# Deadlines of spread-out work that follow TensorE's lag, and the last output chunk computed at the very end in two halves

## The chip, the cores and the metric

The kernel runs on one core of one Trainium2 chip. The metric is device time in microseconds (us) for one execution of the whole program. A core has five engines that work side by side, each through its own queue of instructions in a fixed order: TensorE (PE in the profile, with its weight loads as PEld), VectorE (DVE), ScalarE (ACT), GpSimd (POOL) and SyncE (SP), which here only issues DMA transfers. An instruction that waits for another engine holds up everything behind it in its own queue.

## The reference

For a sequence of 2048 rows with 640 channels, the input is normalised by rows, and three things are added: the input, a state-space convolution of the normalised rows, and a dense layer with a Mish activation.

```
xn = layernorm(x)                                   # x: 2048 x 640
y  = causal_convolution(xn, K) + xn * D_skip        # K from A, C, dt: one kernel per channel
h  = xn @ w1 + b1                                   # w1: 640 x 1728
act = h * tanh(softplus(h))                         # Mish
return x + y + act @ w2                             # w2: 1728 x 640
```

## The kernel before

**Blocks, chunks and products.** The 2048 rows are handled in 4 blocks of 512 (`b` = 0 to 3), the 1728 hidden channels in 14 chunks (`f` = 0 to 13: 128 channels each, chunk 8 only 64), the 640 output channels in 5 chunks of 128 (`k` = 0 to 4). Every float32 product is made of three products of 16-bit parts (high by high, low by high, high by low). For each block and chunk TensorE makes the hidden values (`mm1`, matmul line L770), ACT and DVE turn them into activations (`chain`), and TensorE multiplies them with `w2` and adds them up in five banks `ACC[k]` (`mm2`, L822, 15 matmuls of 512 columns for a full chunk), three chunks later.

**Pairs.** In blocks 1 to 3 chunks (0,1), (2,3), (4,5), (6,7), (9,10) and (11,12) are made in pairs by a scheme with fewer products (`mm1_pair`, L790, matmuls of 256 columns). For each pair TensorE runs five pieces, `one`, `two`, `three_a`, `three_b` and `four`, with pieces of older `mm2` between them. `three_a` (9 matmuls) needs a sum that DVE makes in PSUM (`z`, L1022), `four` needs another (`w`, L1026); ACT makes two copies between `one` and `two` (L1018, L1019). "Pair 3/4" below is the pair of block 3 that begins with chunk 4.

**The chain of a chunk.** Sigmoid (ACT L852), product with it (DVE L856), arctan, square and tanh (ACT L861, L866, L871), product (DVE L876), high part (ACT L883), low part (DVE L894).

**Spread work.** Between all this lies work that is due only much later: the normalisation and splitting of the next block (L621, L535, L580, L587), the convolution as two scans on DVE for each of 5 channel chunks of a block (copies on ACT L706 and L708, scans L712 and L716, sum L726: `ka`, `kb`, `kc`, `ke` in the planner), and 29 checks on the size of the weights (`ck`, ACT L672 and L675, with their loads `lc` on SP). The checks end in a chain of small DVE instructions (`ce`, L682 to L694), a small product on TensorE in the middle of pair 3/9 (L697), and a flag (L700).

**The planner.** The class `Plan` sets the order of instructions on every engine while the program is being built. TensorE's operations stand in one fixed list; each of them is due when the operations before it would end if TensorE never waited (`dues`). Operations of the other engines inherit deadlines backwards from those that need them; spread work also carries an explicit deadline (`due=`). `run` then gives each engine, again and again, the ready operation with the earliest deadline.

**The end.** After the last `mm1` (chunk 13 of block 3) come the `mm2` of chunk 10, then `t 0` (9 matmuls of chunk 11), `t 1` (15 of chunks 11 and 12), and `tail`, which needs chunk 13's activations. In `tail` each output chunk gets its last products, is added to the rows by DVE (`drain`, L899) and stored from SP (L900). Output chunk 4 gets chunk 13's products last, in two halves of 256 columns in two other banks; its bank is added to the rows before that (L1055). SP waits for all stores before the program ends (L1314).

Of the kernel before, what the change touches and what calls it, by code (L numbers as in the profile page):

```python
# [17 lines left out]
OP = mybir.AluOpType  # L18
AX = mybir.AxisListType

P = 128
# [4 lines left out]
TB = 512  # L26
NB = L // TB
NT = TB // P
KD = D // P
FC = [P] * 8 + [64] + [P] * 5  # L30
# [29 lines left out]
class Plan:  # L60
# [26 lines left out]
    def add(self, name, eng, cost, fn, pre=(), take=None, drop=(), due=None, rel=0.0, kb=0.0):  # L87
        assert name not in self.ops, name
        self.ops[name] = o = dict(name=name, eng=eng, cost=cost, fn=fn, pre=[p for p in pre if p not in self.end],
                                  take=take, drop=drop, due=1e9 if due is None else due, rel=rel, kb=kb, n=len(self.ops))  # L90
        if eng == "PE":
            self.pe.append(o)

# [13 lines left out]
    def dues(self):  # L107
        t = self.t["PE"]
        for o in self.pe:
            o["due"] = t + o["cost"]  # L110
            t += o["cost"]
        order, seen = [], set()

        def visit(o):
            stack = [(o, iter(o["pre"]))]
            seen.add(o["name"])
            while stack:
                x, it = stack[-1]
                p = next(it, None)
                if p is None:  # L120
                    order.append(x)
                    stack.pop()
                elif p not in seen:
                    seen.add(p)
                    stack.append((self.ops[p], iter(self.ops[p]["pre"])))

        for o in self.ops.values():
            if o["name"] not in seen:
                visit(o)
        for o in reversed(order):  # L130
            for p in o["pre"]:
                q = self.ops[p]
                if q["eng"] != "PE":
                    wait = 4.0 if q["kb"] else self.GAP[q["eng"]]
                    q["due"] = min(q["due"], o["due"] - o["cost"] - wait)

    def run(self):
        self.dues()
        todo = {e: {} for e in self.t}
        for o in self.ops.values():  # L140
            todo[o["eng"]][o["name"]] = o
        line = list(self.pe)
        while any(todo.values()):
            best = None
            for e, ops in todo.items():
                if not ops:
                    continue
                c = []
                for o in ([line[0]] if e == "PE" else ops.values()):
                    r = self.ready(o)  # L150
                    if r is not None:
                        c.append((max(r, self.t[e]), o))
                if not c:
                    continue
                t0 = min(r for r, _ in c)
                now = sorted((o["due"] - o["cost"], o["n"], o) for r, o in c if r <= t0 + 1e-9)
                late = [(o["due"] - o["cost"], r, o) for r, o in c if r > t0 + 1e-9]
                pick = None
                for u, _, o in now:
                    if not any(w < u and r < t0 + o["cost"] and w < t0 + o["cost"] for w, r, _ in late):  # L160
                        pick = (t0, o)
                        break
                if pick is None:
                    _, r, o = min(late, key=lambda z: (z[1], z[0]))
                    pick = (r, o)
                if best is None or pick[0] < best[0]:
# [253 lines left out]
def body(ctx: ExitStack, tc: tile.TileContext, x, xT, logA, Aim, Cr, Ci, logdt, vec, w1, w1T, w2, w2T, out):  # L420
# [378 lines left out]
    def mm2_ops(f, ks=range(KD), end=False):  # L799
        n = FC[f]  # L800
        hi, lo = ACT[f]
        st, en = f == 0, f == LAST or end
# [15 lines left out]
        return [t for x, y, z in zip(h, m, l) for t in ((*x, False, False), (*y, False, False), (*z, False, en))]  # L818

    def run(ops):  # L820
        for o, w, x, start, stop in ops:
            pe.matmul(o, w, x, start=start, stop=stop)  # L822

    def mm2(f, ks=range(KD), end=False):
        run(mm2_ops(f, ks, end))

    def mm2_last(ks, t=slice(0, TB), to=None):

        hi, lo = (z[:, t] for z in ACT[LAST])
        o = [(ACC[k] if to is None else to)[:, t] for k in ks]  # L830
        for k, z in zip(ks, o):
            c = slice(k * P, (k + 1) * P)
            pe.matmul(z, W2H[LAST][:, c], hi, start=to is not None, stop=False)
            pe.matmul(z, W2L[LAST][:, c], hi, start=False, stop=False)
        for k, z in zip(ks, o):
            pe.matmul(z, W2H[LAST][:, k * P:(k + 1) * P], lo, start=False, stop=True)


    def src(b, f):
# [62 lines left out]
    def whole():  # L902
# [31 lines left out]
        def second(b, f, parts):  # L934
# [7 lines left out]
            for j, (lo, hi) in enumerate(zip([0, *parts], ends)):  # L942
                last = j == len(parts)

                def go(lo=lo, hi=hi):
                    run(mm2_ops(f)[lo:hi])

                more = []
                if f == 0 and b > 0:
                    more = [[("j", b - 1, 0), ("j", b - 1, 1)], [("j", b - 1, k) for k in (2, 3, 4)], []][j]  # L950
                cost = M5 * (min(hi, 15) - lo) if FC[f] == P else 0.17 * (hi - lo)
                ops.append(lambda name=("m2", *n, j), go=go, p=pre + more, d=[("h", *n)] if last else [], cost=cost: add(
                    name, M, cost, go, pre=p, drop=d))
            return ops
# [31 lines left out]
        for b in range(1, NB):  # L986
            for f in range(NF):
# [45 lines left out]
                if i == NP - 1 and b == NB - 1:  # L1033
# [6 lines left out]


        b, k = NB - 1, KD - 1
        add(("t", 0), M, 9 * M5, lambda: mm2(LAST - 2, [4, 3, 2]), pre=[("a4", b, LAST - 2), ("v4", b, LAST - 2)])
        add(("t", 1), M, 15 * M5, lambda: (mm2(LAST - 1, [4], end=True), mm2(LAST - 1, [3]), mm2(LAST - 2, [0]),
                                           mm2(LAST - 1, [0]), mm2(LAST - 2, [1])),
            pre=[("a4", b, LAST - 1), ("v4", b, LAST - 1)])

        def tail(b=NB - 1, k=KD - 1):
# [11 lines left out]
        add(("t", 2), M, 30 * M5, tail, pre=[("a4", b, LAST), ("v4", b, LAST)] + [("ex", b, j) for j in range(KD)])  # L1060


        at = {}
# [277 lines left out]
```

## Time and profile before

| | |
|---|---|
| median of 3 executions | 366.23 us (365.05 to 366.76) |
| the profiled execution | 364.73 us, its span 362.9 us |
| granted TensorE clock | 0.998 |
| busy: PE / DVE / ACT / POOL | 351.1 / 311.4 / 298.3 / 48.8 us |
| chain that ended last | PE 86%, DVE 7%, DMA 3%, ACT 2% |

The span runs from the first to the last instruction; the 1.8 us by which the execution is longer lie outside it. A row of waits names the engine and line that waited, what it waited for, and the total, the count and the longest in us. A row of windows gives, for a stretch of the span, the busy us of each engine. TensorE is busy nearly all the time, so what counts is where it waits, and what lies before its first matmul and behind its last.

### The profile page before, as it was taken

Reading aid. Unit: us, or ns where it says so; the run is one execution under the profiler, and the core shown is the slowest. Engines: PE = TensorE matmul, PEld = TensorE weight load, DVE = VectorE, ACT = ScalarE, POOL = GpSimd, SP = SyncE. Lnnn points to the kernel's source line nnn. Section 1 sums busy time; section 2 is a strip of 40 time slices with the busy share of each in tenths; the row PEclk is TensorE's granted clock in tenths of the full one; section 3 lists DMA queues with packets and bytes.
Section 4 is the critical chain, followed back from the end, with each engine's and each line's share of the span. In section 5 each row is a group of like instructions: output and inputs, shape, how many; then the busy total and the mean of one; then the engine's idle time right before and its main releaser. Section 6 shows DMA issues by size and latency. Waiting matters only on the chain.

```text
span 362.9 us, 6023 instructions
## 1 busy us (share of the span) xinstructions
PE 351.1 (97%) x2161; PEld 210.7 (58%) x2161; DVE 311.4 (86%) x585; ACT 298.3 (82%) x614; POOL 48.8 (13%) x72
## 2 busy tenths in 40 slices
PE   7999999999999999999999999999999979999992
PEld 6754444445666665665666665576556646566541
DVE  5989989999998999999999867999999688885443
ACT  3599999987488699899989797999889986977730
POOL 2100010000032201020104231010003630000000
PEclk9999999999999999999999999999999999999999
DMA  7879975105129908622447942932003973111004
GB/s 231 279 235 286 349 233 189 54 1 181 38 47 194 327 37 209 252 65 54 122 155 153 239 135 64 345 93 67 0 2 58 177 189 72 29 29 31 0 4 151
DMA packets 26037, 48.75 MB, mean 134 GB/s; under 512 B 3577, under 2 KB 6929, under 8 KB 26001
## 3 DMA queue, kind: packets, MB, share of 16 engines
q1 hardware_dynamic: 19152, 34.21, 29.5%
q0 software_dynamic: 6240, 13.11, 17.8%
q10 hardware_dynamic: 608, 0.98, 0.8%
q8 instruction: 19, 0.31, 0.4%
q14 instruction: 18, 0.14, 0.2%
HBM read 39.10 MB, written 5.26 MB: 122 GB/s over the span
## 4 chain that ended last, share of the span: by engine, by line
PE 86%; DVE 7%; DMA 3%; ACT 2%; issue 1%; ACTq 0%
PE acc L822 43%; PE h L790 17%; PE h L770 13%; PE tr L790 10%; DMA w<-in_w_dram 3%; PE h L752 1%; PE tr L752 1%; DVE xl L535 1%; DVE A L856 1%; DVE g L716 1%; DVE lo L894 1%; DVE g L712 1%; DVE tl L587 1%; DVE A L876 0%; DVE t L580 0%
## 5 line engine op out<-in xcount | busy, mean ns | idle before, releaser
L822 PE MATMUL acc<-hi,w2h 128*128 128x512 f16 x275 | 101.6, 379 | 0.0
L822 PE MATMUL acc<-hi,w2l 128*128 128x512 f16 (+1 forms) x267 | 100.5, 379 | 0.0
L822 PE MATMUL acc<-lo,w2h 128*128 128x512 f16 x255 | 94.0, 379 | 0.0
L822 PEld LDWEIGHTS <-w2h 128*128 128x128 f16 x530 | 51.6, 98 | 48.9 <-issue 1.3
L790 PEld LDWEIGHTS <-w1h 128*128 128x128 f16 x432 | 42.3, 98 | 10.7
L852 ACT ACTIVATE s<-h,cv 128x512 f32<-128x512 f32 (+1 forms) x51 | 30.7, 604 | 20.9 <-PE h L790 16.1
L822 PEld LDWEIGHTS <-w2l 128*128 128x128 f16 x275 | 25.8, 98 | 31.3 <-issue 1.6
L876 DVE SCALAR_TENSOR_TENSOR A<-p,A 128x512 f32<-128x512 f32 (+1 forms) x56 | 38.3, 684 | 5.9 <-ACT p L871 5.6
L894 DVE SCALAR_TENSOR_TENSOR lo<-A,hi 128x512 f16<-128x512 f32 x52 | 35.5, 683 | 8.5 <-ACT hi L883 8.3
L883 ACT ACTIVATE hi<-A 128x512 f16<-128x512 f32 (+1 forms) x56 | 34.9, 623 | 7.2 <-DVE A L876 6.9
L861 ACT ACTIVATE p<-s,kc 128x512 f32<-128x512 f32 (+1 forms) x56 | 40.1, 717 | 0.5
L866 ACT ACTIVATE p<-p,kc 128x512 f32<-128x512 f32 (+1 forms) x56 | 40.1, 716 | 0.6
L871 ACT ACTIVATE p<-p,kc 128x512 f32<-128x512 f32 (+1 forms) x56 | 40.1, 716 | 0.5
L856 DVE SCALAR_TENSOR_TENSOR A<-h,bs,s 128x512 f32<-128x512 f32 (+1 forms) x51 | 32.8, 650 | 6.0 <-ACT s L852 5.9
L515 POOL DMA_DIRECT2D r<-in_xT_dram x15 | 13.6, 1075 | 118.6 <-ACT r L733 59.0
L790 PEld LDWEIGHTS <-w1l 128*128 128x128 f16 x216 | 21.1, 98 | 10.7 <-issue 2.7
L770 PEld LDWEIGHTS <-w1h 128*128 128x128 f16 (+1 forms) x174 | 15.3, 99 | 20.3 <-issue 3.3
L716 DVE TENSOR_TENSOR_SCAN g<-g,car,g 128x512 f32<-128x512 f32 x20 | 25.6, 1279 | 0.6
L712 DVE TENSOR_TENSOR_SCAN g<-g,car,kc 128x512 f32<-128x512 f32 x20 | 25.5, 1275 | 0.1
L790 PE MATMUL tr<-xh,w1h 128*128 128x256 f16 x90 | 24.5, 273 | 0.1
L790 PE MATMUL tr<-xl,w1h 128*128 128x256 f16 x90 | 24.5, 273 | 0.0
L790 PE MATMUL tr<-xh,w1l 128*128 128x256 f16 x90 | 24.5, 273 | 0.0
(171 smaller groups left out, 722.8 us busy)
## 6 DMA issues: line engine op xcount, KB each, us to landing
w<-in_w_dram SPq DMA_DIRECT2D x23, 320.0 KB, 4.3
w<-in_w2T_dram SPq DMA_DIRECT2D x15, 288.0 KB, 7.0
w<-in_B_w_dram SPq DMA_DIRECT2D x13, 320.0 KB, 4.7
w<-in_w1T_dram SPq DMA_DIRECT2D x13, 320.0 KB, 7.3
x<-in_A_u_dram SPq DMA_DIRECT2D x12, 320.0 KB, 5.9
xt<-in_xT_dram SPq DMA_DIRECT2D x15, 256.0 KB, 5.7
r<-in_xT_dram POOLq DMA_DIRECT2D x15, 256.0 KB, 5.9
xt<-r POOLq DMA_DIRECT2D x15, 256.0 KB, 4.0
```

The lines of the kernel that those rows point to most:

```text
L716: v.tensor_tensor_scan(g0, g0, g1[:, 0:TB], car[:, 0, k:k + 1], op0=OP.add, op1=OP.add)
L770: pe.matmul(o, w, x, start=(j == 0), stop=(j == len(order) - 1))
L790: pe.matmul(o, p, q, start=start and n == 1, stop=n == 3 * len(w), skip_group_check=True)
L822: pe.matmul(o, w, x, start=start, stop=stop)
L852: a.activation(pl["s", b, f][:n, c], src(b, f) if h is None else h, AF.Sigmoid, bias=cv[:n, f:f + 1], scale=1 / SH)
L856: v.scalar_tensor_tensor(pl["A", b, f][:n, c], src(b, f) if h is None else h, bs[:n, f:f + 1], pl["s", b, f][:n, c], op0=OP.add, op1=OP.mult)
L861: a.activation(pl["p", b, f][:n], pl["s", b, f][:n], AF.Arctan, bias=one[:n], scale=-1.0)
L866: a.activation(p, p, AF.Square, bias=pi4[:n], scale=2.0)
L871: a.activation(p, p, AF.Tanh, bias=mb[:n], scale=MG)
L876: v.scalar_tensor_tensor(A, pl["p", b, f][:n], MC, A, op0=OP.add, op1=OP.mult)
L883: a.activation(hi[:n], A, AF.Copy, scale=MA * SA / SH)
L894: v.scalar_tensor_tensor(lo, A, MA * SA / SH, hi[:n], op0=OP.mult, op1=OP.subtract)
```

## The change

Three things are edited.

1. **Two deadlines for spread work.** The explicit deadline is kept apart as `soft`. `due` now comes only from TensorE's list. In `run`, `lag` is how far TensorE's planned time is behind its list, and an operation's deadline is the earlier of `due` and `soft + lag`. The first deadline of the checks moves from pair 1/6 to pair 1/4, their last from chunk 8 of block 3 to pair 3/11. The planned costs of the pieces of chunk 8's `mm2` and of the end are also given anew.
2. **Output chunk 4 at the very end.** The products of hidden chunks 11, 12 and 13 for output chunk 4 are all made at the end of `tail`, by halves of 256 columns in the two other banks. Its bank `ACC[4]` therefore ends with chunk 10, and is added to the rows as the first DVE instruction of `tail`.
3. **The order of the other products there.** `t 0` and `t 1` are now 6 matmuls each (output chunks 0 and 1); the products of chunks 11 and 12 for output chunks 2 and 3 stand in `tail`.

```diff
@@ Plan.add
-                                  take=take, drop=drop, due=1e9 if due is None else due, rel=rel, kb=kb, n=len(self.ops))
+                                  take=take, drop=drop, due=1e9, soft=1e9 if due is None else due, rel=rel, kb=kb, n=len(self.ops))
@@ Plan.dues
-                    q["due"] = min(q["due"], o["due"] - o["cost"] - wait)
+                    for u in ("due", "soft"):
+                        q[u] = min(q[u], o[u] - o["cost"] - wait)
@@ Plan.run
+            lag = max(0.0, self.t["PE"] - line[0]["due"] + line[0]["cost"]) if line else 0.0
+            until = lambda o: min(o["due"], o["soft"] + lag) - o["cost"]
...
-                now = sorted((o["due"] - o["cost"], o["n"], o) for r, o in c if r <= t0 + 1e-9)
-                late = [(o["due"] - o["cost"], r, o) for r, o in c if r > t0 + 1e-9]
+                now = sorted((until(o), o["n"], o) for r, o in c if r <= t0 + 1e-9)
+                late = [(until(o), r, o) for r, o in c if r > t0 + 1e-9]
@@ body
+    def mm2_half(f, k, o, t, start=False):
+        hi, lo = (z[:, t] for z in ACT[f])
+        c = slice(k * P, (k + 1) * P)
+        pe.matmul(o, W2H[f][:, c], hi, start=start, stop=False)
+        pe.matmul(o, W2L[f][:, c], hi, start=False, stop=False)
+        pe.matmul(o, W2H[f][:, c], lo, start=False, stop=f == LAST)
@@ second
-                cost = M5 * (min(hi, 15) - lo) if FC[f] == P else 0.17 * (hi - lo)
+                cost = M5 * (min(hi, 15) - lo) if FC[f] == P else M5 * (min(hi, 6) - min(lo, 6)) + 0.11 * (max(hi, 6) - max(lo, 6))
@@ the end
-        add(("t", 0), M, 9 * M5, lambda: mm2(LAST - 2, [4, 3, 2]), ...)
-        add(("t", 1), M, 15 * M5, lambda: (mm2(LAST - 1, [4], end=True), mm2(LAST - 1, [3]), mm2(LAST - 2, [0]),
-                                           mm2(LAST - 1, [0]), mm2(LAST - 2, [1])), ...)
+        two, one = LAST - 2, LAST - 1
+        add(("t", 0), M, 6 * M5, lambda: [mm2(two, [j]) for j in range(2)], ...)
+        add(("t", 1), M, 6 * M5, lambda: [mm2(one, [j]) for j in range(2)], ...)
 
         def tail(b=NB - 1, k=KD - 1):
+            v.scalar_tensor_tensor(XT[b][:, k], ACC[k], 1 / SO, XT[b][:, k], op0=OP.mult, op1=OP.add)
             for j in range(k):
-                if j in (1, 2):
-                    mm2(LAST - 1, [j])
+                if j > 1:
+                    mm2(two, [j])
+                    mm2(one, [j])
                 mm2_last([j])
                 drain(b, j, ACC[j])
-                if j == 0:
-                    v.scalar_tensor_tensor(XT[b][:, k], ACC[k], 1 / SO, XT[b][:, k], op0=OP.mult, op1=OP.add)
             for t, to in ((CA, H[0]), (CB, H[1])):
-                mm2_last([k], t, to)
+                mm2_half(two, k, to[:, t], t, True)
+                mm2_half(one, k, to[:, t], t)
+                mm2_half(LAST, k, to[:, t], t)
                 drain(b, k, to, t)
@@ the checks
-        t0, t1 = start(1, 6), start(3, 8)
+        t0, t1 = start(1, 4), start(3, 11)
```

TensorE's order is the same in both kernels up to the end. On the other engines instructions move from the middle of block 1 on. In the rows below the changed kernel's line numbers are up to 11 higher: `z` is L1022 before and L1033 after, `w` L1026 and L1037, the scans L712 and L716 become L715 and L719, the sum behind them L726 becomes L729, and the chain's L856, L876 and L894 become L867, L887 and L905.

DVE from `w` of pair 2/11 on, in the stretch that ends at `z` of pair 3/0. First the kernel before:

```order
L1026 TENSOR_TENSOR h_212<-h_212,pvs 128x256
L894 SCALAR_TENSOR_TENSOR lo_254<-A_246,hi_253 128x512
L535 SCALAR_TENSOR_TENSOR xl_183<-xt,xh_173 128x512
L535 SCALAR_TENSOR_TENSOR xl_185<-xt,xh_175 128x512
L856 SCALAR_TENSOR_TENSOR A_244<-h_211,bs,s_243 128x256
L712 SCALAR_TENSOR_TENSOR g_233<-g_233,car,kc 128x512
L587 SCALAR_TENSOR_TENSOR tl_204<-t_231,th_200 128x512
L716 SCALAR_TENSOR_TENSOR g_234<-g_234,car,g_233 128x512
L621 TENSOR_TENSOR xt<-xt,bc_240 128x512
L726 SCALAR_TENSOR_TENSOR xt<-xt,cc,g_234 128x512
```

The same place after (`g` are the scans' buffers, `xl` the low parts of the next block):

```order
L1037 TENSOR_TENSOR h_212<-h_212,pvs 128x256
L538 SCALAR_TENSOR_TENSOR xl_185<-xt,xh_175 128x512
L905 SCALAR_TENSOR_TENSOR lo_254<-A_246,hi_253 128x512
L867 SCALAR_TENSOR_TENSOR A_244<-h_211,bs,s_243 128x256
L590 SCALAR_TENSOR_TENSOR tl_204<-t_232,th_200 128x512
L624 TENSOR_TENSOR xt<-xt,bc_240 128x512
L583 TENSOR_TENSOR t_230<-xt,t_232 128x512
L624 TENSOR_TENSOR xt<-xt,bc_241 128x512
```

Two scans and their sum (L712, L716, L726), and one of the low parts (L535), have moved ahead of this stretch. Up to `z` of pair 3/0 there are 25 DVE instructions behind `w` before and 23 after: four have gone, and two (an L729 and an L583) have come in from behind `z`.

DVE from `z` to `w` of pair 3/4. First before:

```order
L1022 TENSOR_TENSOR h_211<-h_212,pvs 128x256
L876 SCALAR_TENSOR_TENSOR A_244<-p_248,A_244 128x512
L856 SCALAR_TENSOR_TENSOR A_245<-tr,bs,s_242 128x256
L712 SCALAR_TENSOR_TENSOR g_233<-g_233,car,kc 128x512
L856 SCALAR_TENSOR_TENSOR A_245<-h_211,bs,s_242 128x256
L716 SCALAR_TENSOR_TENSOR g_234<-g_234,car,g_233 128x512
L726 SCALAR_TENSOR_TENSOR xt<-xt,cc,g_234 128x512
L1026 TENSOR_TENSOR h_212<-h_212,pvs 128x256
```

The same place after:

```order
L1033 TENSOR_TENSOR h_211<-h_212,pvs 128x256
L887 SCALAR_TENSOR_TENSOR A_244<-p_248,A_244 128x512
L867 SCALAR_TENSOR_TENSOR A_245<-tr,bs,s_242 128x256
L715 SCALAR_TENSOR_TENSOR g_233<-g_233,car,kc 128x512
L1037 TENSOR_TENSOR h_212<-h_212,pvs 128x256
```

Between the two sums one scan is left of two, and the second L856 and the sum L726 no longer stand ahead of `w`.

DVE around `z` of pair 3/9, where the check chain ends (L694 before and L697 after make `ok`, which the small product on TensorE needs). First before:

```order
L694 TENSOR_TENSOR ok<-ok,z 128x1
L712 SCALAR_TENSOR_TENSOR g_233<-g_233,car,kc 128x512
L716 SCALAR_TENSOR_TENSOR g_234<-g_234,car,g_233 128x512
L726 SCALAR_TENSOR_TENSOR xt<-xt,cc,g_234 128x512
L894 SCALAR_TENSOR_TENSOR lo_252<-A_245,hi_251 128x512
L856 SCALAR_TENSOR_TENSOR A_246<-A_246,bs,s_242 64x512
L1022 TENSOR_TENSOR h_211<-h_212,pvs 128x256
```

The same place after:

```order
L715 SCALAR_TENSOR_TENSOR g_233<-g_233,car,kc 128x512
L1033 TENSOR_TENSOR h_211<-h_212,pvs 128x256
L694 SCALAR_TENSOR_TENSOR c<-q_105 128x4
L867 SCALAR_TENSOR_TENSOR A_244<-tr,bs,s_243 128x256
L694 SCALAR_TENSOR_TENSOR c<-q_105 128x2 x2
L696 TENSOR_REDUCE z<-c 128x1
L697 TENSOR_TENSOR ok<-ok,z 128x1
L719 SCALAR_TENSOR_TENSOR g_234<-g_234,car,g_233 128x512
L1037 TENSOR_TENSOR h_212<-h_212,pvs 128x256
```

`ok` stood six rows ahead of `z`, and stands five rows behind it now.

More of the change, by code (lines that the diff above doesn't have):

```diff
@@ L797, in mm1_pair, with mm2_ops @@
                 lambda: (prod(PY, plain_w(1, 1), sums_x(4)), prod(PY, last_w(1), [(EH, EL)])))
-    def mm2_ops(f, ks=range(KD), end=False):
+    def mm2_ops(f, ks=range(KD), end=[]):
         n = FC[f]
         hi, lo = ACT[f]
-        st, en = f == 0, f == LAST or end
+        st = f == 0
         if n < P:
@@ L817, in mm2_ops @@
             return [t for x, z in zip(h, l) for t in ((*x, True, False), (*z, False, False))] + [(*x, False, False) for x in m]
-        return [t for x, y, z in zip(h, m, l) for t in ((*x, False, False), (*y, False, False), (*z, False, en))]
+        return [t for k, x, y, z in zip(ks, h, m, l) for t in ((*x, False, False), (*y, False, False), (*z, False, f == LAST or k in end))]
     def run(ops):
@@ L822, in run, with mm2, mm2_last @@
             pe.matmul(o, w, x, start=start, stop=stop)
[L824 to L830, printed above, removed]
+    def mm2(f, ks=range(KD)):
+        run(mm2_ops(f, ks))
+    def mm2_last(ks):
+        hi, lo = ACT[LAST]
+        o = [ACC[k] for k in ks]
         for k, z in zip(ks, o):
             c = slice(k * P, (k + 1) * P)
-            pe.matmul(z, W2H[LAST][:, c], hi, start=to is not None, stop=False)
+            pe.matmul(z, W2H[LAST][:, c], hi, start=False, stop=False)
             pe.matmul(z, W2L[LAST][:, c], hi, start=False, stop=False)
@@ L945, in go @@
                 def go(lo=lo, hi=hi):
-                    run(mm2_ops(f)[lo:hi])
+                    run(mm2_ops(f, end=[KD - 1] if (b, f) == (NB - 1, LAST - 3) else [])[lo:hi])
                 more = []
@@ L1042, in whole, with tail @@
         b, k = NB - 1, KD - 1
-        add(("t", 0), M, 9 * M5, lambda: mm2(LAST - 2, [4, 3, 2]), pre=[("a4", b, LAST - 2), ("v4", b, LAST - 2)])
-        add(("t", 1), M, 15 * M5, lambda: (mm2(LAST - 1, [4], end=True), mm2(LAST - 1, [3]), mm2(LAST - 2, [0]),
-                                           mm2(LAST - 1, [0]), mm2(LAST - 2, [1])),
-            pre=[("a4", b, LAST - 1), ("v4", b, LAST - 1)])
-        def tail(b=NB - 1, k=KD - 1):
+        two, one = LAST - 2, LAST - 1
+        add(("t", 0), M, 6 * M5, lambda: [mm2(two, [j]) for j in range(2)], pre=[("a4", b, two), ("v4", b, two)])
+        add(("t", 1), M, 6 * M5, lambda: [mm2(one, [j]) for j in range(2)], pre=[("a4", b, one), ("v4", b, one)])
+        def tail(b=NB - 1):
+            v.scalar_tensor_tensor(XT[b][:, k], ACC[k], 1 / SO, XT[b][:, k], op0=OP.mult, op1=OP.add)
             for j in range(k):
-                if j in (1, 2):
-                    mm2(LAST - 1, [j])
+                if j > 1:
+                    mm2(two, [j])
+                    mm2(one, [j])
                 mm2_last([j])
                 drain(b, j, ACC[j])
-                if j == 0:
-                    v.scalar_tensor_tensor(XT[b][:, k], ACC[k], 1 / SO, XT[b][:, k], op0=OP.mult, op1=OP.add)
             for t, to in ((CA, H[0]), (CB, H[1])):
-                mm2_last([k], t, to)
+                mm2_half(two, k, to[:, t], t, True)
+                mm2_half(one, k, to[:, t], t)
+                mm2_half(LAST, k, to[:, t], t)
                 drain(b, k, to, t)
-        add(("t", 2), M, 30 * M5, tail, pre=[("a4", b, LAST), ("v4", b, LAST)] + [("ex", b, j) for j in range(KD)])
+        add(("t", 2), M, 33 * M5, tail, pre=[("a4", b, LAST), ("v4", b, LAST)] + [("ex", b, j) for j in range(KD)])
         at = {}
```

## The prediction

> **What bounds the kernel now.** I read the page first, then the waits of TensorE, then the busy times by stage. On the page, the busy time of each engine:
>
> ```profile
> span 362.9 us, 6023 instructions
> ...
> PE 351.1 (97%) x2161; PEld 210.7 (58%) x2161; DVE 311.4 (86%) x585; ACT 298.3 (82%) x614; POOL 48.8 (13%) x72
> ```
>
> TensorE is idle for 362.9 - 351.1 = 11.8 us in all. No more than that can be won by an order that leaves its work as it is, and the start and the end hold most of it. The waits of TensorE between 100 and 340 us (who waited for whom; total, times, longest):
>
> ```profile
> PE h L790 <- DVE h L1026: 2.1, 1, 2.1
> PE h L790 <- DVE h L1022: 0.6, 1, 0.6
> ```
>
> There are two waits, each once, both for a half-sum of DVE. Busy us by stage say where (PE, PEld, DVE, ACT, POOL, then clock, DMA share, GB/s):
>
> ```profile
> 20.00:148.00 128.00, 128.00 (x717) 68.80 (x716) 121.67 (x262) 112.12 (x214) 11.33 (x15) 1.00 0.59 174
> 148.00:172.00 24.00, 23.88 (x157) 14.73 (x156) 23.53 (x36) 23.30 (x54) 2.90 (x4) 1.00 0.32 93
> 172.00:200.00 28.00, 28.00 (x189) 18.30 (x188) 26.62 (x46) 25.35 (x57) 5.93 (x7) 1.00 0.57 143
> 200.00:232.00 32.00, 32.00 (x209) 19.80 (x207) 24.81 (x43) 27.27 (x61) 6.76 (x10) 1.00 0.66 173
> 232.00:268.00 36.00, 35.44 (x234) 22.23 (x232) 34.80 (x55) 33.13 (x75) 2.02 (x3) 1.00 0.25 81
> 268.00:290.00 22.00, 22.00 (x150) 14.51 (x149) 18.08 (x30) 20.97 (x45) 9.21 (x12) 1.00 0.56 94
> 290.00:300.00 10.00, 7.89 (x55) 5.14 (x53) 8.25 (x13) 8.68 (x21) 3.37 (x5) 1.00 0.76 191
> ```
>
> TensorE's idle time here is 24.00 - 23.88 = 0.12, 36.00 - 35.44 = 0.56 and 10.00 - 7.89 = 2.11 us, together **2.79 us**. The table also shows a fault of order: DVE is full in 232 to 268 (34.80 of 36), where TensorE waits 0.56 us, while in 200 to 232 it stood idle for 7.19 us.
>
> **Part 1: the deadlines.** The scans and sums that stood between the half-sums are placed elsewhere; nothing is added or removed in all. So TensorE's waits are the term. The larger one, DVE from `z` to `w` of pair 3/4 (start, us, idle before and its cause in brackets):
>
> ```profile
> 289.61 0.43 DVE L1022 TENSOR_TENSOR h<-h,pvs 128x256 f32<-128x256 f32 x1 [1.57 <-PE h L790]
> 289.95 0.68 DVE L876 SCALAR_TENSOR_TENSOR A<-p,A 128x512 f32<-128x512 f32 x1
> 290.55 0.48 DVE L856 SCALAR_TENSOR_TENSOR A<-tr,bs,s 128x256 f32<-128x256 f32 x1
> 291.10 1.28 DVE L712 TENSOR_TENSOR_SCAN g<-g,car,kc 128x512 f32<-128x512 f32 x1
> 294.03 0.48 DVE L856 SCALAR_TENSOR_TENSOR A<-h,bs,s 128x256 f32<-128x256 f32 x1 [1.64 <-ACT s L852]
> 294.43 1.28 DVE L716 TENSOR_TENSOR_SCAN g<-g,car,g 128x512 f32<-128x512 f32 x1
> 295.74 0.75 DVE L726 SCALAR_TENSOR_TENSOR xt<-xt,cc,g 128x512 f32<-128x512 f32 x1
> 296.41 0.43 DVE L1026 TENSOR_TENSOR h<-h,pvs 128x256 f32<-128x256 f32 x1
> ```
>
> `w` starts 6.8 us behind `z`, because an L856 ahead of it waits for ACT, and a scan and a sum follow. In the new order `w` stands right behind the first scan. By these rows that is 291.10 + 1.28 = 292.4, or 2.8 us behind `z`. TensorE asks for it after `three_a`, `three_b` and six matmuls, which take 1.98 us for 18 of 256 columns and 6/15 of 3.24 us by the chain's rows shown further down, 3.3 us in all after `z` has ended at 290.04, so at about 293.3. `w` is done at about 292.8. The 2.1 us go, with 0.5 us to spare.
>
> The smaller wait is `z` of pair 3/0. Behind `w` of pair 2/11 two scans (1.28 each), a sum (0.75) and a low part (about 0.7, as the L876 above) leave the stretch, and a sum and a subtraction (0.75 and about 0.7) come in: 4.0 - 1.45 = 2.6 us less on a DVE that was full. That is over four times the wait of 0.6 us. The work that left has to fit earlier, into blocks 1 and 2; the cover is DVE's idle 28 - 26.62 = 1.38 us and 7.19 us in 172 to 232.
>
> The gain is at most 2.79 us. The bound below is a loss, and is priced as a rival. I take 2.6, leaving 0.2 us for new short waits, the size of the 0.12 us that are left in 148 to 172 where DVE and ACT are as full as they are anywhere (23.53 and 23.30 of 24).
>
> Three things that move along cost nothing by these rows. Loads of the checks stand up to four places earlier in SP's queue, but no wait of TensorE ends with a transfer. GpSimd's adds and stores of a block (13% busy) move by a few places. And the check chain gets late: `ok` was made at 316.0, and its product ran at 325.4:
>
> ```profile
> L694 DVE TENSOR_TENSOR ok<-ok,z x1: 146/146/146, 316.0 to 316.0; 128x1 f32<-128x1 f32 x1
> ```
>
> ```profile
> L697 PE MATMUL tr<-ok,ones x2: 169/210/250, 325.4 to 325.4; 128*128 128x1 f32 x2
> ```
>
> Of these 9.4 us little is left: `ok` now stands behind `z` of the same pair, with one L856 (0.48) and five tiny rows (0.15 to 0.2 each) between, about 1.4 us, while TensorE does 18 matmuls (1.98 us) before the product. So 0.5 us remain, and every us of delay beyond them would be TensorE's.
>
> **Part 2: the end.** The chain in order of time (start, us, what) gives the matmuls' prices, first 256 columns, then 512:
>
> ```profile
> 291.52 1.98 PE h L790 x18
> ...
> 340.36 3.24 PE h L770 x15
> 343.60 8.42 PE acc L822 x39
> ```
>
> A matmul of 256 columns is 1.98/18 = 0.110 us, one of 512 is 0.216. Six full ones become twelve halves: 12 x 0.110 - 6 x 0.216 = +0.02 us, nothing. [...]
>
> The cover of the last chunk's chain shrinks. Its rows, and `tail`'s first matmul:
>
> ```profile
> 343.64 0.69 ACT L852 ACTIVATE s<-h,cv 128x512 f32<-128x512 f32 x1 [0.73 <-PE h L770]
> ...
> 348.38 0.69 DVE L894 SCALAR_TENSOR_TENSOR lo<-A,hi 128x512 f16<-128x512 f32 x1 [0.69 <-ACT hi L883]
> ...
> 351.86 0.38 PE L833 MATMUL acc<-hi,w2h 128*128 128x512 f16 x1
> ```
>
> The chain runs from 343.64 to 349.07, 5.4 us. TensorE fills it with 39 matmuls (8.42 us) now, and with 15 + 6 + 6 = 27 in the new order: 27 x 0.216 = 5.83 us. It still covers, with 0.4 us left. An ACT or DVE step of chunk 12 that slips in between (0.6 to 0.7 us) would cost about 0.2 us; I take nothing.
>
> Then the drains. DVE's and TensorE's last rows, and the last two stores on SP:
>
> ```profile
> 354.00 0.69 DVE L899 SCALAR_TENSOR_TENSOR xt<-acc,xt 128x512 f32<-128x512 f32 x1
> 355.29 1.34 DVE L899 SCALAR_TENSOR_TENSOR xt<-acc,xt 128x512 f32<-128x512 f32 x2 [0.60 <-PE acc L836]
> 356.55 0.74 DVE L899 SCALAR_TENSOR_TENSOR xt<-h,xt 128x256 f32<-128x256 f32 x2
> ```
>
> ```profile
> 356.29 0.27 PE L836 MATMUL h<-lo,w2h 128*128 128x256 f16 x1
> ```
>
> ```profile
> L900 SPq DMA_DIRECT2D out_dram<-xt x2: 402/412/423, 357.1 to 357.6; - x2
> ...
> DMA to landing us min/median/max: 3.5/3.7/3.8
> ```
>
> The last matmul ends at 356.56. Four drains then lie on one another: the last one ends at 356.55 + 0.74 = 357.29, and its store is issued only at 357.6, behind the store before it. With nine half matmuls (0.99 us) to each half, DVE and SP are free when the last drain comes: it runs from 356.6 to about 357.0 (two take 0.74), and its store goes out at once. That is 0.5 us earlier. The landing took 3.5 us with the stores of the other three drains close ahead of it; over all six stores the same view has 2.5 to 3.8:
>
> ```profile
> DMA to landing us min/median/max: 2.5/3.5/3.8
> ```
>
> With the stores spread over 4 us, I take 3.1, between the best and the median, and keep 2.5 and 3.8 as ends. The end thus gains 0.5 + 0.4 = 0.9 us, within 0.2 to 1.5. Behind the landing (357.6 + 3.5 = 361.1) stand 1.8 us to the end of the span that nothing here touches. The added DVE sum at the head of `tail` (0.68 us) ends before the first drain is ready, since three matmuls (0.65 us) and the 0.4 us of spare time lie ahead of that.
>
> **The sum.** 2.6 + 0.9 = 3.5 us. Against the profiled execution that is 364.73 - 3.5 = 361.2, with a span of 359.4. The median of the runs shown, 366.23, lies 1.5 us above the profiled one; taking the same 3.5 us from it gives **362.7 us**, and that is the forecast (1.0% faster). A measurement of this kernel tells about 0.5% (1.8 us) from no change.
>
> **Rivals.** *New short waits take the place of the old ones.* With TensorE no longer late, its pieces meet DVE and ACT with half a microsecond to spare, as for `w` of pair 3/4 and for `ok`. Should two or three such meetings miss by the length of one scan or check step (0.7 to 1.3 us), 1.5 to 2.5 us come back, and 1.0 to 2.0 us of gain are left: 364.2 to 365.2. For it speaks that ACT and DVE are over 90% busy in half the stages; against it that TensorE met only two waits of any weight in the 18 pairs before.
>
> *The work that was moved forward does not fit (slower).* Place: DVE from 172 to 232 and again in 268 to 290. By counting rows of both orders, with 1.28 for a scan and 0.6 to 0.75 for the rest, up to 4.3 us of DVE work more lie ahead of `w` of pair 2/9, and after most of that has been evened out at pair 3/2 another 2.4 us ahead of `z` of pair 3/4. If none of it found idle DVE time, TensorE would wait 6.7 us and the kernel take 366.23 - 3.5 + 6.7 = 369.4; it is slower than before once more than 3.5 of the 6.7 us find no room. DVE's idle time of 8.6 us and 22 - 18.08 = 3.9 us in these stages speaks against it; that idle time bound to waits for ACT cannot be filled speaks for it.
>
> *The deadlines do nothing where TensorE waits, and only the end gains.* Then it is 366.23 - 0.9 = 365.3. The two orders shown are against it, since both places have changed.
>
> **How the numbers follow.** The forecast's case gets 0.66, new short waits 0.16, the slower rival 0.12 (most of it over 0.5% slower), only the end 0.06. The first gives 361.6 (2.79 + 1.5 us, and 0.3 us for the runs) to 363.9; 8 in 10 of all needs some of the second and third case too, and the spread of the medians shown, so the range is 361.2 to 365.8. Faster by over 0.5% (below 364.4) is the first case and a small part of the second: 0.67. Within 0.5% come most of the second, the fourth and a little of the slower rival: 0.21. Slower by over 0.5%: 0.12.
>
> **What would show it.** Right: no wait of TensorE for L1037 or L1033 over 0.3 us, TensorE's idle time from 20 us to its last matmul below 0.5 us, the last drain 0.1 us behind the last matmul, its store landing within 3.1 us or so, and a span near 359.4. Wrong in part 1: waits of TensorE for ACT's copies, for a low part (L905) or for `ok`, or for half-sums in block 2. Wrong in part 2: a wait at `tail`'s first matmul, or a landing of 3.5 us or more.

## The result and the profile after

The changed kernel takes **359.88 us** (median of six runs, 359.29 to 360.67) against 365.64 us (364.85 to 366.76) for the kernel before on the same chip: a ratio of 0.9842 [0.9817, 0.9866], 1.6% faster. The prediction had the sign, but 359.88 lies below its range (361.2 to 365.8). The profiled execution of the changed kernel took 359.29 us with a span of 357.5; that of before took 364.73 with 362.9. All lines of "after" below come from that one execution.

The page, span and busy us by engine:

```profile
span 357.5 us, 6018 instructions
...
PE 350.6 (98%) x2167; PEld 211.5 (59%) x2167; DVE 311.1 (87%) x585; ACT 296.3 (83%) x614; POOL 50.4 (14%) x72
```

No engine's work changed by more than 2 us; TensorE's idle time fell from 11.8 to 6.9 us. Among TensorE's waits between 100 and 340 us there is no row left. Busy us by stage (columns as in the prediction):

```profile
200.00:232.00 32.00, 32.00 (x208) 19.66 (x206) 27.25 (x41) 27.98 (x63) 9.77 (x13) 1.00 0.72 187
232.00:268.00 36.00, 36.00 (x239) 22.90 (x238) 34.74 (x58) 32.59 (x72) 0.00 (x0) 1.00 0.21 72
268.00:290.00 22.00, 22.00 (x149) 14.29 (x147) 18.59 (x28) 20.63 (x48) 9.13 (x11) 1.00 0.63 114
290.00:300.00 10.00, 10.00 (x72) 6.87 (x71) 9.04 (x12) 8.39 (x20) 3.79 (x5) 1.00 0.74 173
```

DVE's work in 200 to 232 us rose from 24.81 to 27.25 us without holding up TensorE: what moved forward found room. The half-sum `w` of pair 3/4 now stands here (DVE's row, then two of TensorE, from the timeline):

```profile
291.39 0.43 DVE L1037 TENSOR_TENSOR h<-h,pvs 128x256 f32<-128x256 f32 x1 [0.31 <-PE h L793]
```

```profile
293.25 0.38 PE L825 MATMUL acc<-hi,w2l 128*128 128x512 f16 x1
293.47 0.27 PE L793 MATMUL h<-th,w1h 128*128 128x256 f16 x1
```

`w` ends at 291.82, and its first reader starts at 293.47, straight behind the matmul before it: 1.65 us to spare.

The end, in the timeline (DVE's three last drains, TensorE's last matmul) and in the view of the store's line, its last two stores:

```profile
351.23 0.69 DVE L910 SCALAR_TENSOR_TENSOR xt<-acc,xt 128x512 f32<-128x512 f32 x1 [1.25 <-PE acc L839]
352.21 0.42 DVE L910 SCALAR_TENSOR_TENSOR xt<-h,xt 128x256 f32<-128x256 f32 x1 [0.29 <-PE h L847]
353.19 0.42 DVE L910 SCALAR_TENSOR_TENSOR xt<-h,xt 128x256 f32<-128x256 f32 x1 [0.56 <-PE h L847]
```

```profile
352.88 0.27 PE L847 MATMUL h<-lo,w2h 128*128 128x256 f16 x1
```

```profile
L911 SPq DMA_DIRECT2D out_dram<-xt x2: 332/508/683, 352.7 to 353.6; - x2
...
DMA to landing us min/median/max: 2.1/2.2/2.4
```

DVE now sits idle before each of the three drains and each runs as soon as its matmuls are done. The last matmul ends at 352.88 + 0.27 = 353.15, the last drain runs 0.04 us later, and its store goes out at 353.6.

The last line is of the two half stores together: the first of them landed in 2.4 us, the last one in 2.1. In the kernel before it was 3.8 and 3.5.

**Where 5.4 us went** (span 362.9 to 357.5; the issue of the last store from SP's timeline, 357.60 before and 353.64 after):

| | before | after | gain |
|---|---|---|---|
| last matmul ends | 356.56 | 353.15 | 3.41 |
| from there to the issue of the last store | 1.04 | 0.49 | 0.55 |
| landing of the last store | 3.5 | 2.1 | 1.4 |
| behind the landing, from span and landing | 1.8 | 1.8 | 0.0 |

The first line holds the waits of TensorE, and they were longer than the busy table says. The last matmul ahead of the larger one and the first behind it, in the timeline of before:

```profile
294.40 0.38 PE L822 MATMUL acc<-hi,w2l 128*128 128x512 f16 x1
...
296.89 0.27 PE L790 MATMUL h<-th,w1h 128*128 128x256 f16 x1 [2.11 <-DVE h L1026]
```

The row calls TensorE busy for 0.38 us, but unhindered the next matmul would have started 0.216 us later. From start to start TensorE lost 296.89 - 294.40 - 0.22 = 2.27 us, not 2.11. Counted so, the wait at pair 3/0 is 0.72 (not 0.56), there are 0.22 at 161.5 and 0.09 at 278, and together 3.30 us are gone; the work itself started 0.11 us earlier.

### The profile page after: what moved, and what is told of

Same layout as the page of the kernel before. It is cut to its first block, busy times and chain, and to the rows that moved or that the text cites. A ratio compares the mean times of both kernels' runs of the same rounds, so it can differ in the third digit from the quotient of the medians.

```text
span 357.5 us, 6018 instructions
## 1 busy us (share of the span) xinstructions
PE 350.6 (98%) x2167; PEld 211.5 (59%) x2167; DVE 311.1 (87%) x585; ACT 296.3 (83%) x614; POOL 50.4 (14%) x72
## 4 chain that ended last, share of the span: by engine, by line
PE 95%; DMA 1%; DVE 1%; SPq 0%; ACT 0%; issue 0%; DVEq 0%
PE acc L825 48%; PE h L793 18%; PE h L773 14%; PE tr L793 12%; DMA x<-in_A_u_dram 1%; PE h L755 1%; PE tr L755 1%; PE acc L1217 0%; PE acc L839 0%; PE acc L836 0%; PE acc L837 0%; DVE w1l L526 0%; DVE st L598 0%; SPq L1236 0%; DVE st L597 0%
## 5 line engine op out<-in xcount | busy, mean ns | idle before, releaser
L887 DVE SCALAR_TENSOR_TENSOR A<-p,A 128x512 f32<-128x512 f32 (+1 forms) x56 | 38.2, 682 | 7.2 <-ACT p L882 7.0
L905 DVE SCALAR_TENSOR_TENSOR lo<-A,hi 128x512 f16<-128x512 f32 x52 | 35.3, 680 | 3.6 <-ACT hi L894 3.3
L867 DVE SCALAR_TENSOR_TENSOR A<-h,bs,s 128x512 f32<-128x512 f32 (+1 forms) x51 | 33.0, 647 | 6.2 <-ACT s L863 6.0
L894 ACT ACTIVATE hi<-A 128x512 f16<-128x512 f32 (+1 forms) x56 | 34.9, 624 | 3.6 <-DVE A L887 3.4
L715 DVE TENSOR_TENSOR_SCAN g<-g,car,kc 128x512 f32<-128x512 f32 x20 | 25.6, 1278 | 1.1 <-ACT g L709 1.1
L719 DVE TENSOR_TENSOR_SCAN g<-g,car,g 128x512 f32<-128x512 f32 x20 | 25.5, 1276 | 0.1
```

The lines of the kernel that those rows point to most:

```text
L715: v.tensor_tensor_scan(g1[:, 1:], g1[:, 1:], zero.to_broadcast([P, TB]), car[:, 1, k:k + 1], op0=OP.add, op1=OP.add)
L867: v.scalar_tensor_tensor(pl["A", b, f][:n, c], src(b, f) if h is None else h, bs[:n, f:f + 1], pl["s", b, f][:n, c], op0=OP.add, op1=OP.mult)
L887: v.scalar_tensor_tensor(A, pl["p", b, f][:n], MC, A, op0=OP.add, op1=OP.mult)
L894: a.activation(hi[:n], A, AF.Copy, scale=MA * SA / SH)
L905: v.scalar_tensor_tensor(lo, A, MA * SA / SH, hi[:n], op0=OP.mult, op1=OP.subtract)
```

## The experiments

Ten kernels ran. Unless it says "on the changed kernel", an edit is made on the kernel before. In all of them line numbers shift a little with the edit.

**The two parts apart.** First the planning alone, with the old end:

```diff
 # Plan.add / dues / run: soft deadlines that move with TensorE's lag (as in the change)
-                cost = ... else 0.17 * (hi - lo)
+                cost = ... else M5 * (min(hi, 6) - min(lo, 6)) + 0.11 * (max(hi, 6) - max(lo, 6))
-        t0, t1 = start(1, 6), start(3, 8)
+        t0, t1 = start(1, 4), start(3, 11)
```

> All edits of the planner (lag rule, window of the checks, costs of chunk 8's products), the old end. Theory A (two separate gains: TensorE's waits of 3.3 us counted from start to start, and 2.0 us behind the last matmul): TensorE's waits go, the last matmul ends near 353.2 instead of 356.6, the stretch behind it stays 6.3 us, and the time falls by 3.4 us (0.9%). Rival B (the end alone was late because the kernel was late; the stores land faster once the planner's order is changed): the stretch behind the last matmul also falls below 5 us, and the time falls by over 4.5 us.

It took 361.83 us (361.38 to 362.43) against 365.29: 0.9901 [0.9878, 0.9925]. Its last matmul and its last drains, in the timeline:

```profile
352.85 0.27 PE L839 MATMUL h<-lo,w2h 128*128 128x256 f16 x1
```

```profile
351.86 1.34 DVE L902 SCALAR_TENSOR_TENSOR xt<-acc,xt 128x512 f32<-128x512 f32 x2 [0.60 <-PE acc L839]
353.11 0.74 DVE L902 SCALAR_TENSOR_TENSOR xt<-h,xt 128x256 f32<-128x256 f32 x2
```

The median falls by 3.5 us, as Theory A has it. The matmuls end at 353.12, as early as in the changed kernel (353.15), and the drains lie on one another as before. So the 3.4 us belong to the planning alone, and all that the new end gives lies behind the last matmul.

Then the new end alone, with the old order ahead of it:

```diff
 # mm2_ops, mm2_last, mm2_half, ("t", 0..2) and tail as in the change; Plan, cost line and t0, t1 as before
```

> Only the end is changed; all orders before it stay. Theory A: both waits for the half-sums (2.1 and 0.6 us) stay, the last matmul ends near 356.5, and the stretch behind it falls from 6.3 to about 4.4 us: 2.0 us (0.5%) less. Rival C (my term of the prediction, a landing of 3.1 us; the 2.2 us landings of the changed kernel are luck): 0.9 us less.

Its median, 364.46 us, looks like a small gain: 0.996 [0.9941, 0.9979]. But its twelve executions fall in two groups, five at 362.76 to 363.26 and seven at 364.43 to 365.49. The profile is of an execution of the upper group. Windows around the 2.1 us wait, which this kernel keeps (the column behind POOL's is TensorE's granted clock), and TensorE's rows there:

```profile
294.40:297.10 2.70, 0.59 (x4) 0.19 (x3) 2.67 (x5) 2.63 (x6) 0.00 (x0) 1.00 0.53 147
297.10:300.30 3.20, 3.20 (x13) 1.82 (x13) 2.70 (x4) 2.66 (x8) 1.45 (x2) 0.50 0.54 93
300.30:304.00 3.70, 3.70 (x24) 2.25 (x23) 2.92 (x4) 2.17 (x6) 0.89 (x1) 0.97 0.16 64
```

```profile
297.09 0.37 PE L790 MATMUL h<-th,w1h 128*128 128x256 f16 x1 [2.11 <-DVE h L1034]
297.26 0.42 PE L790 MATMUL h<-th,w1l 128*128 128x256 f16 x1
297.47 0.42 PE L790 MATMUL h<-tl,w1h 128*128 128x256 f16 x1
```

After the wait the clock is 0.50 for 3.2 us, only 13 matmuls run in that time, and those of 256 columns soon start 0.21 us apart instead of 0.11. The profiled execution of before had the same wait at a clock of 1.00, 28 matmuls in 3.5 us:

```profile
297.00:300.50 3.50, 3.50 (x28) 2.55 (x27) 3.50 (x5) 3.17 (x8) 1.36 (x2) 1.00 0.61 132
```

The kernel before has two groups too: of the 23 executions beside these experiments 15 lie at 364.58 to 365.61 (median 364.94) and 8 at 366.18 to 367.68. Lower group against lower group (median 363.08), the new end alone gains 1.9 us, and upper against upper (366.60 and 364.55) 2.0, as Theory A has it. By the two medians it would be 0.8, near the 0.9 of Rival C; but the medians mix the groups in different shares (seven of 12 in the upper one here, eight of 23 before). Against the same lower group the planning alone gains 3.1 us and the whole change (359.88) 5.1, so the two parts add up.

**The planning taken apart.** The lag rule alone:

```diff
+            lag = max(0.0, self.t["PE"] - line[0]["due"] + line[0]["cost"]) if line else 0.0
+            until = lambda o: min(o["due"], o["soft"] + lag) - o["cost"]
 # with "soft" in add and dues; cost line and t0, t1 as before
```

> Only the rule that spread work's deadlines move with TensorE's lag; the window of the checks, the costs and the end stay as before. Theory D (the rule itself removes the waits): waits for the half-sums go, about 3 us (0.8%) less. Rival E (the order depends on every number of the planner, and only the three edits together fit): other waits of 0.3 to 1 us come up, and the gain is under 1.5 us.

362.33 us (361.81 to 363.37), 0.9915 [0.989, 0.994], as Theory D has it. One wait is left, and the last matmul ends at 354.04, so this rule alone gives 2.5 of the 3.4 us:

```profile
PE h L793 <- DVE h L1025: 0.3, 1, 0.3
```

```profile
353.77 0.27 PE L839 MATMUL h<-lo,w2h 128*128 128x256 f16 x1
```

The other two numbers alone:

```diff
-                cost = ... else 0.17 * (hi - lo)
+                cost = ... else M5 * (min(hi, 6) - min(lo, 6)) + 0.11 * (max(hi, 6) - max(lo, 6))
-        t0, t1 = start(1, 6), start(3, 8)
+        t0, t1 = start(1, 4), start(3, 11)
```

> The window of the checks and the costs of chunk 8's products as in the changed kernel, no lag rule, the old end. Theory D: the waits stay, within 0.7 us of the time before. Rival E: some of the waits go and others come up (for chunk 9's activations in block 2, for the flag's check chain in pair 3/9), a gain between 0 and 2.5 us.

364.07 us (363.77 to 364.54), 0.9954 [0.9937, 0.9972]. The two old waits are gone, and four others have come, as Rival E has it:

```profile
PE acc L822 <- DVE hi L894: 0.4, 1, 0.4
PE acc L822 <- ACT hi L883: 0.4, 1, 0.4
PE acc L822 <- DVE lo L894: 0.3, 1, 0.3
PE tr L697 <- DVE ok L694: 0.3, 1, 0.3
```

And the cost line alone:

```diff
-                cost = ... else 0.17 * (hi - lo)
+                cost = ... else M5 * (min(hi, 6) - min(lo, 6)) + 0.11 * (max(hi, 6) - max(lo, 6))
```

> The kernel before with only the planned costs of chunk 8's three pieces altered (by 0.5 us in all in each block). Rival E (the old waits belong to one particular order, and any small change of the planner's numbers makes other ones): the 2.1 us wait for w of pair 3/4 is gone, other waits of 0.3 to 1.5 us are there, at z of pair 3/0 above all; time within 1.5 us of before. Theory D (the waits come from the rule that ignores the lag): both waits stay, time unchanged within 0.5 us.

366.91 us (365.19 to 367.68), 1.0031 [1.001, 1.0053]: no faster, by its median slower. The wait for `w` of pair 3/4 is gone, and three others stand at other places, as Rival E has it, though the longest is longer than its 1.5 us. Behind the longest of them the clock halves in the profiled execution:

```profile
PE h L790 <- DVE tl L587: 2.4, 1, 2.4
PE acc L822 <- DVE lo L894: 0.5, 1, 0.5
PE h L790 <- DVE h L1022: 0.4, 1, 0.4
```

```profile
269.40:272.40 3.00, 2.97 (x15) 2.11 (x15) 2.85 (x6) 1.79 (x5) 0.00 (x0) 0.50 0.03 5
```

Its ten executions fall in two groups again, three at 365.19 to 365.53 and seven at 366.82 to 367.68. This is the prediction's rival of new waits, true of parts of the change: each piece moves waits about, and only the orders with the lag rule lose most of them. That this comes from the rule's reason, and not from its being one more order, is not shown: the last two kernels lost both old waits without the rule, against Theory D of their expectations. What speaks for the rule is that its two orders have waits of 0.3 us and of none in all, and the kernel before and the three orders without it (the next experiment is one) have 1.1 to 3.3 us.

**One wait removed, and put back.** The old order, changed at one place only: two steps of DVE may not start before `w` of pair 3/4.

```diff
-  add(("v1", *n), V, 0.38, ..., pre=[("sg", *n), ("vX", *n)], drop=...)
+  add(("v1", *n), V, 0.38, ..., pre=[("sg", *n), ("vX", *n)] + ([("w", *n)] if n == (3, 4) else []), drop=...)
-  add(("kc", c, k), V, 1.2, skip_c, c, k, pre=[("kb", c, k)])
+  add(("kc", c, k), V, 1.2, skip_c, c, k, pre=[("kb", c, k)] + ([("w", 3, 4)] if (c, k) == (3, 0) else []))
```

> The kernel before, with one place altered: the second product of pair 3/4 and the second scan of channel chunk 0 of block 3 wait for the half-sum w of pair 3/4, so that w stands ahead of them on DVE. Theory F (the wait was one misplaced instruction, and it also costs clock): the 2.1 us wait goes, 2.3 us from start to start; the times lose the upper group near 366.6 and lie near 362.7, about 0.7% below the median before. Rival G (DVE is behind with its work, and the wait only moves): a wait of 1 to 1.5 us for w of pair 3/6 takes its place, 1 us or less is gained.

363.85 us (363.25 to 364.64) against 365.59, 0.9948 [0.9929, 0.9967], in one group. The wait of 2.1 us is gone, and a smaller one came further on, beside the one at pair 3/0:

```profile
PE h L790 <- DVE h L1022: 0.6, 1, 0.6
PE h L790 <- DVE h L1026: 0.5, 1, 0.5
```

So this falls between the two expectations: part of the wait moved (0.69 us from start to start), and the upper group went. Against the lower group of before, run beside it (median 364.76), the gain is 0.9 us, as by the last matmul, which ends at 355.71 instead of 356.56; the rest of the 1.7 us between the medians is the upper group's going.

The reverse, on the changed kernel: `w` of pair 3/4 is summed 12 times over, so that TensorE waits for it again. A repeat took 0.47 us where the expectation had assumed about 0.35, so the wait came out as 3.4 us instead of 2.1; the same with 7 and with 9 sums followed for that reason:

```diff
-  add(("w", *n), V, 0.38, lambda: v.tensor_tensor(PW, PY, PVS, op=OP.add), pre=[("three_a", *n)])
+  add(("w", *n), V, 0.38, lambda n=n: [v.tensor_tensor(PW, PY, PVS, op=OP.add)
+      for _ in range(12 if n == (3, 4) else 1)], pre=[("three_a", *n)])
```

> The changed kernel with the half-sum w of pair 3/4 made twelve times over (the same sum to the same place), about 3.8 us of DVE more, of which 1.65 us are hidden. Theory F: TensorE waits about 2.1 us there again; in some executions the clock granted afterwards falls to about a half for some 3 us, which costs 1.6 us more, so the times fall into two groups, about 2.3 and 3.9 us above the changed kernel's 359.9. Rival H (the clock fell in one profile by chance, not by the wait): one group, 2.3 us above.

> The changed kernel with the half-sum w of pair 3/4 made seven times over. Each repeat took 0.47 us with twelve, so TensorE waits 6 x 0.47 - 1.65 = 1.2 us there, from start to start. [...]

> The same with nine sums: 8 x 0.47 - 1.65 = 2.1 us of wait, about that of the kernel before. Theory F: two groups again, near 362.0 and 363.6 us, about half of the executions in each. [...]

The waits of TensorE in the three kernels, in the order of 12, 7 and 9 sums:

```profile
PE h L793 <- DVE h L1037: 3.4, 1, 3.4
```

```profile
PE h L793 <- DVE h L1037: 1.0, 1, 1.0
```

```profile
PE h L793 <- DVE h L1037: 2.0, 1, 2.0
```

The windows behind them, with the granted clock, in the same order:

```profile
297.00:300.40 3.40, 3.21 (x15) 1.73 (x15) 3.40 (x6) 1.45 (x4) 0.01 (x1) 0.68 0.00 0
```

```profile
296.00:300.00 4.00, 4.00 (x27) 2.39 (x25) 4.00 (x6) 3.37 (x9) 0.90 (x1) 1.00 0.30 49
```

```profile
296.00:300.00 4.00, 4.00 (x17) 2.04 (x16) 4.00 (x7) 2.39 (x6) 0.90 (x1) 0.57 0.05 8
```

| sums | wait | from start to start | all executions, us | over 359.88 |
|---|---|---|---|---|
| 7 | 1.0 | 1.21 | 360.56 to 361.64 (5) | 1.1 (median) |
| 9 | 2.0 | 2.14 | 361.77, 361.94, 362.00; 363.36, 363.40, 363.70, 363.82 | 2.1 and 3.7 (medians of the groups) |
| 12 | 3.4 | 3.54 | 363.67; eight at 364.68 to 365.10; 365.55, 366.38, 366.62 | 5.0 (median) |

Against the kernel before, run beside each, the ratios are 0.989 [0.9866, 0.9913] with 7 sums, 0.9935 [0.9911, 0.9959] with 9 and 0.9982 [0.9961, 1.0002] with 12. The 359.88 were not run beside these three, so a few tenths are not to be read. A wait of 1.0 us costs its own length. One of 2.0 us costs its own length in three executions, and 1.6 us more in four. One of 3.4 us costs 1.5 us more than its length from start to start in the median, nothing more in one execution of twelve, and about 3 us more in two, of which there is no profile. The mean granted clock that each execution shows falls with the group: with 9 sums it is 0.999 to 1.000 in the lower group and 0.993 to 0.995 in the upper one, with the new end alone 0.999 to 1.000 and 0.994 to 0.995. In the two windows above behind the wait of the new end alone (0.50 over 3.2 us, 0.97 over the next 3.7) 1.6 + 0.1 = 1.7 us of full clock are missing, which lowers the mean over 363 us by 0.0047. The profiles of the upper groups (the new end alone, the cost line alone, 9 sums) show the half clock, and that of before, from the lower group, does not. So the two groups are taken for executions without and with the half clock behind the waits of 2.0 to 2.4 us.

**The landing.** Why does the last store land in 2.1 us? The expectation of the next run asks whether the stores just ahead of it slow it down. It is the planning-only kernel, whose four last stores go out close together, without two of them:

```diff
-         sp.dma_start(out[...], z)
+         if k not in (2, 3):
+             sp.dma_start(out[...], z)
```

> The planner's edits with the old end (as the first experiment), and the stores of output chunks 2 and 3 of the last block left out, so that only the two half stores are under way at the end. Theory K (the last stores land late because 0.6 MB of other stores lie ahead of them): the last stores land in 2.2 to 2.5 us instead of 3.8, and the time is 1.3 us below that of the first experiment, 360.5. Rival L (they land late because they are issued right behind one another on SP): they still take 3.5 us or more, and the time is within 0.4 us of 361.8.

Landings of the two half stores in us (last column of the DMA view between 346 and 362 us, the middle of the two), for before, planning only, planning only with two stores fewer, the new end alone, and the changed kernel:

```profile
out_dram<-xt SPq DMA_DIRECT2D x2, 128.0 KB, 3.7
```

```profile
out_dram<-xt SPq DMA_DIRECT2D x2, 128.0 KB, 3.8
```

```profile
out_dram<-xt SPq DMA_DIRECT2D x2, 128.0 KB, 2.8
```

```profile
out_dram<-xt SPq DMA_DIRECT2D x2, 128.0 KB, 2.5
```

```profile
out_dram<-xt SPq DMA_DIRECT2D x2, 128.0 KB, 2.2
```

The last store alone landed in 3.5, 3.6, 2.7, 2.4 and 2.1 us, in the same order. With two stores fewer the kernel took 360.96 us (360.81 to 362.05), 0.9883 [0.9849, 0.9918]: 0.87 us less than with them (0.7 by the two ratios, which the intervals do not separate), and its last landing is 0.9 us shorter. That lies between the two expectations, nearer Theory K: most of the slow landing (0.9 of the 1.5 us from 3.6 to 2.1) is the crowd of stores ahead. The remaining 0.6 us, from 2.7 to 2.1, were not taken apart; the two half stores go out 0.4 us apart in that kernel and 1.0 us apart in the changed one. Each landing is from one profile, and the new end gave 2.4 in one and 2.1 in the other.

## Why the prediction was right and wrong

**Right, the places.** Both waits named went, by the planning (3.4 us) as the larger term. The end gained only behind the last matmul. The halves cost nothing: TensorE's end is 353.15 with them and 353.12 without. The last chunk's chain stayed covered; the chain of waits in the changed kernel runs through it without a pause:

```profile
340.18 5.83 PE acc L825 x27
346.01 0.22 PE acc L836
```

340.18 + 5.83 = 346.01: the 27 matmuls took the 5.83 us worked out, and `tail`'s first one follows at once. The slower rival did not come: the work moved forward fits, by the table of stages. New short waits did not come in the whole change, though they did in parts of it.

**Wrong, the bound of the waits.** "TensorE's idle time here is ... together 2.79 us" and "The gain is at most 2.79 us": the measured gain of the planning is 3.4 us, 3.3 of them waits. The step that failed is idle time as stage minus busy time. A matmul's row is 0.16 us longer than its share of the time (0.38 against 0.216), so each wait hides that much, and waits under 0.16 us do not show at all. Then 0.2 us were taken off for new waits, which did not come. Together the term was 0.8 us too small.

**Wrong, the landing.** "I take 3.1, between the best and the median, and keep 2.5 and 3.8 as ends": it was 2.1. The shortest landing of the six stores of before was taken for a lower end, although it belonged to one of the four stores of twice the size (both half stores took 3.5 or more). The step from the old landing to the new one was 1.4 us, not 0.4, so this term was 1.0 us too small; most of it is that fewer stores go out close ahead, as the run without two stores shows (0.9 us). Issuing the store earlier was sized at 0.5 and measured 0.55, so the rest of the end came out as worked out.

**Wrong, the carry to the median.** "The median of the runs shown, 366.23, lies 1.5 us above the profiled one; taking the same 3.5 us from it." The 1.5 us are the difference between the two groups: the three runs shown had a median in the upper one, the profiled execution belongs to the lower one. With the 2.1 us wait the half clock goes as well, so the changed kernel's median lies 0.6 us above its profiled execution. That made 0.9 of the 2.8 us by which 362.7 missed 359.88; the other 1.9 us are the terms above (3.5 forecast, 5.4 measured). The profiled execution had a clock of 1.00 behind the wait, so nothing in it showed this.

**Wrong, but without effect, the two narrow margins.** For `w` of pair 3/4 "0.5 us to spare" came out as 1.65. DVE's `z` of that pair and TensorE's first matmul of `three_a`, in the timeline after:

```profile
288.47 0.43 DVE L1033 TENSOR_TENSOR h<-h,pvs 128x256 f32<-128x256 f32 x1 [0.18 <-PE h L793]
```

```profile
290.21 0.27 PE L793 MATMUL h<-th,swh 128*128 128x256 f16 x1
```

`w` starts at 291.39, 2.9 us behind `z`, as worked out (2.8). But TensorE was in the middle of output matmuls when `z` ended at 288.90, and began `three_a` only at 290.21. The sum let it begin at once, and these 1.3 us are what was missing in it.

For `ok` "0.5 us remain" came out as 2.4 from start to start, where before had 9.4, and for the same reason: `z` of pair 3/9 ended at 318.72, and TensorE began `three_a` only at 320.03, again 1.3 us later.

```profile
L697 DVE TENSOR_TENSOR ok<-ok,z x1: 160/160/160, 319.6 to 319.6; 128x1 f32<-128x1 f32 x1
```

```profile
L700 PE MATMUL tr<-ok,ones x2: 169/210/250, 322.0 to 322.0; 128*128 128x1 f32 x2
```

## What to carry to other kernels

Count a wait of the bounding engine from the start of the instruction before it to the start of the one behind it, less the usual spacing; the idle time between busy rows is too small, here by 0.16 us for each wait. Where a median lies far from the profiled execution, look at the single times for two groups before carrying the difference over: a wait that costs the clock afterwards is worth more than its length (here a wait of 2.0 us cost 1.6 us more in four of seven executions). For the last store of a kernel, use the landing of a store with nothing close ahead of it (here 2.1 us against 3.5), and put work between the drains rather than behind them.

## What the hardware showed

**A wait can cost the clock behind it.** With a wait of 1.0 us of TensorE, the clock stayed at 1.00 in the profile and all five times lie in one group. With 2.0 us four of seven executions were in the upper group, with 2.1 us 24 of 63 (before: 8 of 23, 13 of 28, 3 of 12) and seven of 12 (the new end alone), and with 2.4 us seven of ten. With 3.4 us the median lies 1.5 us above what the wait alone explains. In the four profiles with the loss the clock was 0.50 for 3.0 to 3.4 us, by the spacing of the matmuls (0.21 us instead of 0.11 for 256 columns) and by the windows. With waits of 2.1 and 2.4 us the wide spacing began with the first matmuls behind the wait. With 3.4 us nine matmuls ran 0.11 us apart first, and it began 1.0 us behind the wait. With 2.0 us the 0.57 over the 4.0 us from 296.00 on is 3.4 us at half clock; the windows on either side are at 1.00, so it began 0.2 to 0.8 us behind the wait. In all, the waits of 2.0 to 2.4 us had it in 42 of 92 executions, counted by the upper groups. What decides between the two in an execution was not shown.

**Crowding of small stores.** The same 128 KB store from SP landed in 2.1 and 2.4 us when the stores ahead were spread, in 3.5 and 3.6 us close behind two others and its pair, and in 2.7 us with those two left out.
